# Banded attention and a cosine-gated MLP on one core: value differences in the first two blocks, paired bursts, later weight sums

## The chip, the core and the metric

The program runs on one core of one Trainium2 chip. The metric is the device time of one execution in microseconds; the kernel before takes 678.24 us (median of three runs, 677.9 to 679.14). The engines are named as the profile names them: PE multiplies matrices (PEld loads its weights), DVE, ACT and POOL work on vectors, SP issues the transfers.

## What is computed

Attention over a band of 96 keys and 8 global keys, for 4 batches of 8 heads, 768 positions and 64 columns, and then a two-layer network over all 3072 tokens of 512 columns with 2048 hidden ones:

```python
scores = scale * np.matmul(q, k.transpose(0, 1, 3, 2))
keep = is_global | is_local          # pos < 8, or 0 <= rel < 96
scores = np.where(keep, scores + bias, -1e9)
a = np.exp(scores - np.max(scores, axis=-1, keepdims=True))
x = np.matmul(a / (np.sum(a, axis=-1, keepdims=True) + 1e-09), v)
h = x @ w_in
out = (h * np.cos(h)) @ w_out
```

Inputs are float32; the kernel multiplies each matrix as a high and a low part, in three products.

## The kernel before

**Tiling.** The queries are cut into blocks of 96. A *part* is a run of blocks of one batch: batch 0 has parts 0 and 1 of four blocks each (`OPEN`), each later batch has parts of three, three and two blocks (`BLOCKS`), parts 2 to 10. A *unit* is one part and one pair of heads, so a part has four units. `plan_unit` makes the scores of a unit (lines 663 and 667), folds the two 96-key windows into one (line 685), takes row minima (694), the exponentials with their sums (ACT, 719), adds 1e-9 to the sums (DVE, 727), inverts them (730) and normalises by groups of two blocks (743 and 748, on POOL or DVE). `plan_values` transposes the probabilities on PE (847), copies them from PSUM into two halves of a `pv` tile, and multiplies them by V in a *burst* (`av`, line 890) that uses 64 columns of the array for each head.

**Two ways to split the probabilities.** After the fold one column holds a key of the block before or one of the own block, by the mask `own`. Without differences (parts 0 to 3) DVE makes two masked copies: `others` (line 858) and `own` (864). With differences (`DIFFER`, parts 4 to 10) the first half is a plain copy (`every`, line 855, ACT or DVE, shown as line 297 or 299), the second is `own`, and its products use V of the own block less V of the block before (`vd`, line 821, POOL or DVE). `vd` has one slot, `pv` has three.

**Bursts.** The parts of two blocks put two units into one burst (`both`, `off`), the others one. A burst's result goes to a PSUM bank `px`, from which `plan_x` makes the high part of x (ACT, 297) and the low one (DVE, 938). From part 4 on the attention has two banks ("att"); parts 1 to 3 have three ("wide").

**The network.** `plan_opening` and `plan_step` multiply x by `w_in` (line 973), make the cosine on ACT and DVE (991 to 1104) and multiply by `w_out` (986). From part 3 on, a tile of 256 tokens is multiplied in seven products instead of eight (`plan_fast`, line 1191), with sums of weights that `plan_combined` makes once (lines 496 to 522), stores in DRAM and reads back. `plan_weight` converts the weights from 64-bit words in six steps on ACT, DVE and POOL; line 456 (`wjoin`) puts the words together and 466 (`wrest`) is the last step. `plan_store` copies a finished tile of the plain steps to an `oo` tile and stores it; its slot is of class "wu" for part numbers under `FAST` = 3, else "oo". "wu" is two of the four slots "late", which the sums and the fast steps use as well; "oo" has two slots.

**Order.** All engines take their instructions in the order of a list that `Plan.run` writes: each operation has a cost for every engine that may do it, a due time, slots for its buffers, and a place on the engine that is free first. In the first 110 us (`HURRY`) ACT's costs count half and DVE's double. Where the plan finds a gap on PE in the first 45 us, it puts in products of zeros (line 1518). These stand in no data path.

Of the kernel before, what the change touches and what calls it, by code (L numbers as in the profile page):

```python
# [18 lines left out]
ALU = mybir.AluOpType  # L19
# [7 lines left out]
R = 96  # L27
# [9 lines left out]
UB = 1  # L37
# [11 lines left out]
PE, ACT, DVE, POOL, SP = "PE", "ACT", "DVE", "POOL", "SP"  # L49
# [14 lines left out]
FAST = 3  # L64
SUMS = -5

MERGE = tuple(range(11, 11))
DIFFER = tuple(range(4, 11))
# [3 lines left out]
TAIL = 0.8  # L72

# [32 lines left out]
class Plan:  # L106
# [12 lines left out]
    def __init__(self, places, free):  # L119
        self.ops = []  # L120
        self.places = {c: list(v) for c, v in places.items()}
        self.busy = {}
        self.free = dict(free)
        self.port = 0
        self.mode = None
        self.last = {}

# [5 lines left out]
    def op(self, engines, emit, after=(), uses=(), due=None, table=None, extra=0, port=False, mode=None):  # L133
        o = Op(engines, emit, after, list(uses), due, table, extra, port, mode)
        for a in o.after:
            a.then.append(o)
        for u in o.uses:
            u.users += 1
        self.ops.append(o)
        return o  # L140
# [13 lines left out]
    def run(self):  # L154

        self.dues()
        for i, o in enumerate(self.ops):
            o.key = (o.due - min(o.engines.values()), i)
# [114 lines left out]
class Net:  # L273
# [143 lines left out]
    def plan_weight(self, src, out, at, place, n, due):  # L417

        nc, p = self.nc, self.plan
        raw = Slot(f"w {place}", lambda i: self.const.tile([P, n, 2], U32, name="raw", tag=i))  # L420
# [53 lines left out]
        o = p.op({DVE: part(600)}, wjoin, [o], [raw, wu], port=True)  # L474
        o = p.op({ACT: part(525), DVE: part(335), POOL: part(595)}, whigh, [o], [raw, wu], port=True)
        return p.op({DVE: part(600), POOL: part(1260)}, wrest, [o], [raw, wu], due=due, port=True)

    def plan_combined(self, q):
# [11 lines left out]
        done = [[x] + self.prev.get("sums", []) for x in done]  # L490
# [99 lines left out]
    def plan_unit(self, L, pr):  # L590
# [134 lines left out]
        def add(e):  # L725
            x = st.tile[:, n2 : 2 * n2]
            nc.vector.tensor_scalar(x, x, 1e-9, None, op0=ALU.add)

        def rec(e):
            nc.vector.reciprocal(st.tile[:, 2 * n2 : 3 * n2], st.tile[:, n2 : 2 * n2])  # L730

        o = p.op({DVE: 85}, add, exps, [st], port=True)
        o = p.op({DVE: 120}, rec, [o], [st], port=True)
        u["norm"] = []
        for ts in groups:
            h, na = ts[0], 2 * len(ts)

            def norm(e, h=h, na=na):
                x = tt[h // 2].tile.rearrange("p t j w -> p (t j) w")[:, :na]
                r = st.tile[:, 2 * n2 + 2 * h : 2 * n2 + 2 * h + na].rearrange("p (c o) -> p c o", o=1)  # L740
                if lead(h):
                    for a, w in ((0, R), (2, SLOT)):
                        self.eng(e).tensor_tensor(
                            x[:, a : a + 2, :w], x[:, a : a + 2, :w],
                            r[:, a : a + 2].broadcast_to([R, 2, w]), op=ALU.mult,
                        )
                    return
                self.eng(e).tensor_tensor(x, x, r.broadcast_to([R, na, SLOT]), op=ALU.mult)  # L748
# [51 lines left out]
    def plan_values(self, u):  # L800
# [18 lines left out]
        def step(e):  # L819
            x = vs.tile[:R, :, hs]  # L820
            self.eng(e).tensor_tensor(
                vd.tile[:, pos + lead0 : pos + nb], x[:, lead0 + 1 : nb + 1], x[:, lead0:nb], op=ALU.subtract)
# [6 lines left out]
        for ts in u["groups"]:  # L829
# [37 lines left out]

            def whole(e, pt=pt, pv=pv):
                self.copy(e, pv.tile[:R, 1, : 2 * R], pt.tile[:R, : 2 * R])
# [7 lines left out]
            ready.append(p.op({DVE: 70 + w * 104 // 100}, own, [o], [pt, pv]))  # L877
# [28 lines left out]
        def burst(e):  # L906
# [4 lines left out]
            {PE: 160 * (2 * nb - u["first"]) * len(units)}, burst, [o for x in units for o in x[3]],  # L911
# [87 lines left out]
    def plan_step(self, s, m, q, a, b):  # L999
# [10 lines left out]
        for i in range(2):  # L1010
            f = 2 * q + i
            for kk in range(self.NK):

                def m1(e, kk=kk, f=f, i=i):
# [3 lines left out]
                    {PE: 348}, m1, self.xdone[m, kk] + [self.wdone[f][0]], [ph, *xs, self.weight["wi", f]],  # L1018
# [100 lines left out]
    def plan_fast(self, s, m, q, rr, gg, product, g, due):  # L1119
# [54 lines left out]
        for i, (bank, half, left, right, k) in enumerate(jobs):  # L1174
# [12 lines left out]
            def times(e, b=b, half=half, left=left, right=right, ends=half == 1 or bank == "D"):  # L1187
# [7 lines left out]
                {PE: 348}, times, after, uses + side, due=due + (i + 1) * 348,  # L1195
# [65 lines left out]
    def plan_store(self, m, t, po, o, keep, due):  # L1261
# [3 lines left out]
        if before is not None:  # L1265
            oo = before[0]
        else:
            cls = "part" if keep else "wu" if m < FAST else "oo"
            oo = Slot(cls, lambda i: self.work.tile([P, 512], F32, name="oo", tag=i))
# [175 lines left out]
    def windows(self):  # L1445
# [17 lines left out]
        self.weight, self.saved, self.stored = {}, {}, {}  # L1463
        p = self.plan
# [13 lines left out]
        for n in self.order:  # L1478
            for b2 in range(self.NP // UB):
                L = self.plan_loads(n, b2)  # L1480
                for i in range(UB):
                    self.plan_values(self.plan_unit(L, b2 * UB + i))
        for f in range(self.NF):
            self.wdone[f] = self.plan_weights(f)
        for q in range(NQ):
            self.plan_combined(q)
        for s, (n, i, a, b) in enumerate(self.seq):
            (self.plan_opening if n < len(OPEN) else self.plan_step)(s, n, i, a, b)
        flag = self.plan_flag()
# [105 lines left out]
```

## Time and profile before

| | before |
|---|---|
| median of three runs | 678.24 us |
| span of the profiled execution | 676.7 us |
| PE busy | 663.8 us (98%) |
| DVE busy | 554.6 us (82%) |
| ACT busy | 508.7 us (75%) |
| POOL busy | 391.0 us (58%) |

The span runs from the first to the last instruction; the run's time has 1.5 us around it. A matmul's record lasts longer than the step from its start to the next one's, since matmuls overlap: to see what PE spends on one, subtract starts. In a timeline a row is a run of equal instructions: start, time from the first start to the last end, and how many. The brackets give the idle time before it and what ended that.

### The profile page before, as it was taken

To read this page: it belongs to the slowest core of one execution; us is meant where nothing else is said; L and a number is where in the kernel's file an instruction comes from. 1 tells how busy PE (TensorE), PEld (TensorE's weight loads), DVE (VectorE), ACT (ScalarE), POOL (GpSimd) and SP (SyncE) were. 2 spreads that over 40 slices of the span, in tenths; PEclk is the share of its full clock that TensorE was granted. 3 is DMA by queue.
4 is the path that set the end of the run, shared out by engine and by line. 5 is a ranking of instruction groups with operands and counts; after the bars stand their busy time and mean duration, and the time that the engine had idled before them with its cause. 6 is when DMAs were issued, how large, how long until landed. Compare 5 with 4: busy or idle time off the path is not lost. (4 is left out here: it accounts for less than half of the span.)

```text
span 676.7 us, 17496 instructions
## 1 busy us (share of the span) xinstructions
PE 663.8 (98%) x5810; PEld 626.7 (93%) x5810; DVE 554.6 (82%) x1726; ACT 508.7 (75%) x1253; POOL 391.0 (58%) x576
## 2 busy tenths in 40 slices
PE   8999999999999999999999999999999999999995
PEld 4769999999999998999999999999999999999995
DVE  7999898978898897777778888797878898887664
ACT  7999997579776785866778878676787788684432
POOL 5896544437457553467866776736876768532201
PEclk9999999999999999999999999999999999999999
DMA  8999200044546665877887867787687777665664
GB/s 279 336 321 380 80 1 1 22 159 121 163 139 194 221 183 174 239 220 203 244 240 207 249 213 231 245 239 232 210 240 219 235 228 235 199 224 187 191 226 150
DMA packets 86291, 136.69 MB, mean 202 GB/s; under 512 B 9904, under 2 KB 33968, under 8 KB 86192
## 3 DMA queue, kind: packets, MB, share of 16 engines
q1 hardware_dynamic: 86048, 135.23, 64.7%
q8 instruction: 48, 0.79, 0.5%
q14 instruction: 51, 0.42, 0.2%
q10 hardware_dynamic: 144, 0.26, 0.1%
HBM read 118.67 MB, written 16.78 MB: 200 GB/s over the span
## 5 line engine op out<-in xcount | busy, mean ns | idle before, releaser
L973 PE MATMUL bank<-xmem,w 128*128 128x256 f32 (+1 forms) x2112 | 344.4, 295 | 0.1
L973 PEld LDWEIGHTS bank<-xmem,w 128*128 128x128 f32 x2112 | 294.1, 189 | 7.7 <-issue 0.9
L719 ACT ACTIVATE tt<-tt,st 96x104 f32<-96x104 f32 (+1 forms) x256 | 94.6, 371 | 7.2 <-DVE st L694 6.5
L997 ACT ACTIVATE rr<-rr,half_pi 128x512 f32<-128x512 f32 (+1 forms) x104 | 71.6, 691 | 23.3 <-DVE rr L994 22.1
L986 PE MATMUL bank<-w,gh 128*128 128x256 f32 (+1 forms) x384 | 88.3, 320 | 0.0
L991 ACT ACTIVATE rr<-bank 128x512 int32<-128x512 f32 (+1 forms) x104 | 57.9, 558 | 30.9 <-PE bank L973 29.1
L1191 PE MATMUL bank<-ws,sh 128*128 128x256 f32 x384 | 75.8, 284 | 1.3 <-DVE oo L299 1.3
L994 DVE SCALAR_TENSOR_TENSOR rr<-rr,bank 128x512 f32<-128x512 int32 (+1 forms) x104 | 66.5, 639 | 8.2 <-ACT rr L991 7.6
L784 POOL TENSOR_TENSOR qk<-raw,qk 64x304 fp32r<-64x304 f32 (+1 forms) x57 | 50.0, 880 | 28.4 <-ACT qk L297 6.9
L748 POOL TENSOR_TENSOR tt<-tt,st 96x416 f32<-96x416 f32 (+1 forms) x60 | 45.4, 764 | 35.3 <-DVE sf L1137 9.1
L986 PEld LDWEIGHTS bank<-w,gh 128*128 128x128 f32 x384 | 62.7, 188 | 1.1
L1030 DVE TENSOR_TENSOR rr<-bank,rr 128x512 f32<-128x512 f32 x72 | 49.3, 684 | 16.6 <-ACT rr L997 16.4
L986 PE MATMUL bank<-w,gl 128*128 128x256 f32 (+1 forms) x192 | 61.1, 318 | 0.0
L1191 PEld LDWEIGHTS bank<-ws,sh 128*128 128x128 f32 x384 | 58.6, 188 | 2.0 <-issue 1.4
L297 ACT CAST gh<-rr 128x384 fp32r<-128x384 f32 (+1 forms) x76 | 39.5, 520 | 25.8 <-DVE rr L1030 10.8
L694 DVE CUSTOM_DVE_ANT_0 tt<-bank,dd 96x104 f32<-96x104 f32 (+1 forms) x256 | 55.0, 256 | 2.2
L1191 PE MATMUL bank<-ws,sl 128*128 128x256 f32 x192 | 54.1, 282 | 0.1
L997 ACT ACT_TABLE_LOAD x40 | 51.3, 1283 | 0.7
L719 ACT ACT_TABLE_LOAD x39 | 50.0, 1283 | 0.7
L445 POOL TENSOR_SCALAR raw<-raw 128x512 bf16<-128x512 bf16 (+1 forms) x32 | 36.6, 1167 | 23.6 <-DVE w L466 13.2
L667 PE MATMUL bank<-qk 128*96 128x200 f32 (+1 forms) x384 | 49.1, 257 | 0.0
L1191 PE MATMUL bank<-w,gh 128*128 128x256 f32 x256 | 48.7, 282 | 0.0
(137 smaller groups left out, 1532.4 us busy)
## 6 DMA issues: line engine op xcount, KB each, us to landing
ws<-sum SPq DMA_DIRECT2D x256, 256.0 KB
raw<-in_qk_dram SPq DMA_DIRECT2D x48, 174.0 KB
raw<-in_w_in_dram SPq DMA_DIRECT2D x16, 512.0 KB
sum<-sw SPq DMA_DIRECT2D x64, 128.0 KB
raw<-in_qk_dram SPq DMA_DIRECT2D x48, 150.0 KB
raw<-in_qk_dram SPq DMA_DIRECT2D x48, 148.0 KB
out_dram<-oo SPq DMA_DIRECT2D x23, 256.0 KB
raw<-in_w_out_dram SPq DMA_DIRECT2D x16, 256.0 KB
```

The lines of the kernel that those rows point to most:

```text
L667: nc.tensor.matmul(out, qs[:, m, q0], ks[:, k : k + w], start=m == 0, stop=m == 1)
L694: nc.vector.tensor_tensor_reduce(tt[t // 2].tile[:, t % 2, j, :w], ps.tile[:R, i * WIN : i * WIN + w], self.dd[:, v, :w], op0=ALU.add, op1 ...
L719: nc.scalar.activation(x, x, AF.Exp, bias=st.tile[:, c : c + 1], scale=-1.0, accum_out=st.tile[:, n2 + c : n2 + c + 1])
L748: self.eng(e).tensor_tensor(x, x, r.broadcast_to([R, na, SLOT]), op=ALU.mult)
L784: self.eng(e).tensor_tensor(ks[D:, k0:k1], raw.tile[D:, k0:k1], ks.bitcast(F32)[D:, k0:k1], op=ALU.subtract)
L973: self.nc.tensor.matmul(ph, self.wi[f][:, w, kk * P : (kk + 1) * P], xx[:, kk, :], start=kk == 0 and m == 0, stop=kk == self.NK - 1 and m ...
L986: self.nc.tensor.matmul(out, gg, w[:, i, :], start=start and m == 0 and h == 0, stop=stop and m == 2)
L991: self.nc.scalar.activation(r.bitcast(I32), ph, AF.Copy, scale=1.0 / TWO_PI, bias=0.25)
L994: self.nc.vector.scalar_tensor_tensor(r, r.bitcast(I32), -TWO_PI, ph, op0=ALU.mult, op1=ALU.add)
L997: self.nc.scalar.activation(r, r, AF.Sin, bias=self.half_pi)
L1030: {DVE: dve(512)}, lambda e: nc.vector.tensor_tensor(r(), h(), r(), op=ALU.mult), [o], [ph, rr],
L1191: nc.tensor.matmul(out, x, y, start=q == 0 and j == 0 and half == 0, stop=q == self.NF // 2 - 1 and j == 2 and ends)
```

## The change

- `DIFFER` takes in parts 0 and 1, so that their probabilities are split with value differences. `step` counts V's blocks from the first that is loaded.
- `APART`: in parts 0 and 1 the sums and reciprocals are made for each group of two blocks, each after its own four exponentials, and not once for the unit's eight.
- `MERGE`: parts 2 to 10 pair two units in a burst. In the parts of three blocks the second unit has a bank of its own; the odd blocks of both share a `pv` tile.
- `BEHIND`: in the plan the first weight sum waits for the last 24 joins.
- Part 2 stores from slots of class "oo".
- The planner counts 354 ns for a group of three products instead of 348, and 168 instead of 160 for a pair of products with V.
- Names of operations, `ORDER` and `COPIED` are added; they are empty.

```diff
-MERGE = tuple(range(11, 11))
-DIFFER = tuple(range(4, 11))
+BEHIND = -24
+MERGE = tuple(range(2, 11))
+DIFFER = (0, 1) + tuple(range(4, 11))
+COPIED = ()
+APART = (0, 1)
...
+ORDER = {}
...
-            o.key = (o.due - min(o.engines.values()), i)
+            o.key = (o.due - min(o.engines.values()) + ORDER.get(o.name, 0), i)
...
         o = p.op({DVE: part(600)}, wjoin, [o], [raw, wu], port=True)
+        self.joined.append(o)
...
-        done = [[x] + self.prev.get("sums", []) for x in done]
+        done = [[x] + self.prev.get("sums", self.joined[BEHIND:]) for x in done]
...
-        def add(e):
-            x = st.tile[:, n2 : 2 * n2]
+        def add(e, a, b):
+            x = st.tile[:, n2 + a : n2 + b]
             nc.vector.tensor_scalar(x, x, 1e-9, None, op0=ALU.add)
 
-        def rec(e):
-            nc.vector.reciprocal(st.tile[:, 2 * n2 : 3 * n2], st.tile[:, n2 : 2 * n2])
-
-        o = p.op({DVE: 85}, add, exps, [st], port=True)
-        o = p.op({DVE: 120}, rec, [o], [st], port=True)
+        def rec(e, a, b):
+            nc.vector.reciprocal(st.tile[:, 2 * n2 + a : 2 * n2 + b], st.tile[:, n2 + a : n2 + b])
+
+        ends = None
         u["norm"] = []
         for ts in groups:
             h, na = ts[0], 2 * len(ts)
+            if n in APART or ends is None:
+                cs = (2 * h, 2 * h + na) if n in APART else (0, n2)
+                ends = [x for ((t, _), _), x in zip(ttr, exps) if t in ts or n not in APART]
+                o = p.op({DVE: 85}, lambda e, cs=cs: add(e, *cs), ends, [st], port=True)
+                o = p.op({DVE: 120}, lambda e, cs=cs: rec(e, *cs), [o], [st], port=True)
...
-                vd.tile[:, pos + lead0 : pos + nb], x[:, lead0 + 1 : nb + 1], x[:, lead0:nb], op=ALU.subtract)
+                vd.tile[:, pos + lead0 : pos + nb], x[:, lead0 + 1 - low : nb + 1 - low], x[:, lead0 - low : nb - low], op=ALU.subtract)
...
-            {PE: 160 * (2 * nb - u["first"]) * len(units)}, burst, [o for x in units for o in x[3]],
+            {PE: 168 * (2 * nb - u["first"]) * len(units)}, burst, [o for x in units for o in x[3]],
...
-                    {PE: 348}, m1, self.xdone[m, kk] + [self.wdone[f][0]], [ph, *xs, self.weight["wi", f]],
+                    {PE: 354}, m1, self.xdone[m, kk] + [self.wdone[f][0]], [ph, *xs, self.weight["wi", f]],
...
-                {PE: 348}, times, after, uses + side, due=due + (i + 1) * 348,
+                {PE: 354}, times, after, uses + side, due=due + (i + 1) * 348,
...
-            cls = "part" if keep else "wu" if m < FAST else "oo"
+            cls = "part" if keep else "wu" if m < FAST - 1 else "oo"
```

## Rows read from the trace of the kernel before

**Rows 1.** page section 1: busy us (share of the span) xinstructions.

```profile
PE 663.8 (98%) x5810; PEld 626.7 (93%) x5810; DVE 554.6 (82%) x1726; ACT 508.7 (75%) x1253; POOL 391.0 (58%) x576
```

**Rows 2.** busy time by stretch: us, busy us (x instructions) of each engine.

```profile
0.00:62.00 62.00, 58.34 (x556) 41.30 (x557) 54.65 (x258) 57.20 (x191) 47.01 (x82) 1.00 0.96 324
60.00:80.00 20.00, 20.00 (x143) 18.69 (x143) 17.47 (x31) 20.00 (x43) 10.06 (x11) 1.00 0.64 215
```

**Rows 3.** the same for line 1518 alone, 5.75 to 62 us.

```profile
5.75:62.00 56.25, 9.74 (x38) 3.35 (x38) 1.00 1.00 342
```

**Rows 4.** timeline of PE, opening: start us, us, engine line, operation [idle before].

```profile
8.49 3.41 PE L1518 MATMUL idle<-zeros 128*128 128x512 bf16 x15
12.05 0.51 PE L847 MATMUL bank<-ident,tt 96*96 96x96 f32 x4
29.93 1.83 PE L973 MATMUL bank<-xmem,w 128*128 128x384 f32 x9
```

**Rows 5.** timeline of PE round one burst, 468.9 to 470.9 us.

```profile
468.99 0.28 PE L1191 MATMUL bank<-ws,sl 128*128 128x256 f32 x1
469.10 0.51 PE L973 MATMUL bank<-xmem,w 128*128 128x256 f32 x3
469.54 0.56 PE L890 MATMUL bank<-pv,v 96*64 96x96 f32 x8
470.09 0.34 PE L890 MATMUL bank<-pv,v 104*64 104x96 f32 x4
470.26 0.34 PE L890 MATMUL bank<-pv,vd 96*64 96x96 f32 x4
470.52 0.50 PE L1191 MATMUL bank<-w,sh 128*128 128x256 f32 x2
```

**Rows 6.** timeline of PE, two waits of transposes.

```profile
285.93 0.54 PE L847 MATMUL bank<-ident,tt 96*104 96x96 f32 x4 [0.23 <-POOL tt L748]
...
321.72 0.35 PE L847 MATMUL bank<-ident,tt 96*104 96x96 f32 x2 [0.71 <-DVE pv L299]
```

**Rows 7.** timelines of ACT, SP's queue, DVE and PE, 263 to 271 us.

```profile
263.57 0.59 ACT L297 COPY oo<-bank 128x512 f32<-128x512 f32 x1
264.66 5.69 SPq L1283 DMA_DIRECT2D out_dram<-oo  x2
269.27 0.69 DVE L299 COPY oo<-bank 128x512 f32<-128x512 f32 x1 [1.92 <-DMA out_dram<-oo]
270.11 0.48 PE L1191 MATMUL bank<-ws,sh 128*128 128x256 f32 x2 [1.27 <-DVE oo L299]
```

**Rows 8.** timelines of DVE and POOL, last join and first weight sum.

```profile
129.91 0.42 DVE L456 SCALAR_TENSOR_TENSOR wu<-raw 128x256 uint32<-128x256 uint32 x1
132.51 0.75 POOL L496 TENSOR_TENSOR sw<-w 128x256 f32<-128x256 f32 x1 [0.80 <-DVE qk L774]
```

**Rows 9.** instructions by line, DVE, 0 to 62 us: busy us, mean ns | idle before.

```profile
L858 DVE SCALAR_TENSOR_TENSOR pv<-own,bank 104x384 f32<-104x384 f32 (+1 forms) x16 | 7.9, 496 | 1.4 <-PE bank L847 0.8 <-ACT pv L297 0.4
L730 DVE RECIPROCAL st<-st 96x8 f32<-96x8 f32 x8 | 1.6, 195 | 0.1
L727 DVE TENSOR_SCALAR st<-st 96x8 f32<-96x8 f32 x8 | 1.4, 174 | 0.3 <-ACT tt L719 0.3
```

**Rows 10.** instructions by line and shape, ACT and POOL, whole span.

```profile
L297 ACT COPY pv<-bank 104x384 f32<-104x384 f32 x15 | 7.1, 476 | 3.7 <-DVE pv L864 3.6
L297 ACT COPY pv<-bank 104x192 f32<-104x192 f32 x18 | 5.4, 318 | 4.7 <-PE bank L847 2.5 <-DVE pv L864 2.0
L821 POOL TENSOR_TENSOR vd<-v 96x384 f32<-96x384 f32 x7 | 7.1, 1011 | 4.3 <-PE bank L667 2.9 <-PE bank L973 1.3
```

**Rows 11.** timelines of ACT and POOL, first unit.

```profile
8.70 0.18 ACT L719 ACTIVATION_READ_ACCUMULATOR tt<-tt,st 96x1 f32 x1
10.15 0.19 ACT L719 ACTIVATION_READ_ACCUMULATOR tt<-tt,st 96x1 f32 x1
11.05 0.99 POOL L743 TENSOR_TENSOR tt<-tt,st 96x192 f32<-96x192 f32 x2 [2.20 <-ACT tt L719]
```

More of the change, by code (lines that the diff above doesn't have):

```diff
@@ L126, in __init__ @@
         self.last = {}
+        self.part, self.count = "", {}
     def drained(self, o, e):
@@ L134, in op @@
         o = Op(engines, emit, after, list(uses), due, table, extra, port, mode)
+        name = emit.__name__
+        if name == "<lambda>":
+            self.count[self.part] = self.count.get(self.part, 0) + 1
+            name = f"op{self.count[self.part]}"
+        o.name = f"{self.part} {name}"
         for a in o.after:
@@ L419, in plan_weight @@
         nc, p = self.nc, self.plan
+        p.part = place
         raw = Slot(f"w {place}", lambda i: self.const.tile([P, n, 2], U32, name="raw", tag=i))
@@ L866, in own, with mine @@
                 )
+            def mine(e, pv=pv, a=a, na=na, z0=z0):
+                self.eng(e).tensor_tensor(
+                    wide(pv.tile[:R, 1, z0:], a, na), wide(pv.tile[:R, 0, z0:], a, na), mask(self.own[:R], a, na), op=ALU.mult
+                )
             def whole(e, pt=pt, pv=pv):
@@ L876, in plan_values @@
                 ready.append(p.op({DVE: 70 + w * 104 // 100}, others, [o], [pt, pv]))
-            ready.append(p.op({DVE: 70 + w * 104 // 100}, own, [o], [pt, pv]))
+            if n in COPIED:
+                ready.append(p.op({DVE: 70 + w * 104 // 100, POOL: 100 + w * 1125 // 512}, mine, ready[-1:], [pv], port=True))
+            else:
+                ready.append(p.op({DVE: 70 + w * 104 // 100}, own, [o], [pt, pv]))
             if lead:
@@ L1463, in windows @@
         self.weight, self.saved, self.stored = {}, {}, {}
+        self.joined = []
         p = self.plan
@@ L1479, in windows @@
             for b2 in range(self.NP // UB):
+                p.part = f"v{n}.{b2}"
                 L = self.plan_loads(n, b2)
                 for i in range(UB):
+                    p.part = f"u{n}.{b2 * UB + i}"
                     self.plan_values(self.plan_unit(L, b2 * UB + i))
         for f in range(self.NF):
+            p.part = f"w{f}"
             self.wdone[f] = self.plan_weights(f)
         for q in range(NQ):
+            p.part = f"c{q}"
             self.plan_combined(q)
         for s, (n, i, a, b) in enumerate(self.seq):
+            p.part = f"s{s}"
             (self.plan_opening if n < len(OPEN) else self.plan_step)(s, n, i, a, b)
+        p.part = "flag"
         flag = self.plan_flag()
```

## The prediction

> **What bounds the kernel now.** I read the page's busy shares first, then the busy time by stretch, then the timeline of PE. The reader is to see that PE is busy 98% of the span [rows 1]: nearly every microsecond that another engine saves is worth nothing unless PE gets its work sooner or has less of it. The profiled execution spans 676.7 us, and the median of the runs is 678.24 us, so some 1.5 us lie outside the span; I make the sum on the span's rows and subtract it from the median.
>
> The stretches say where PE's time is not useful work. From 60 us on PE is full (20.00 of 20 us to 80 us) [rows 2], and by the page's 98% nearly so to the end: what is saved there has to be PE's own time, or one of a few waits. In the first 62 us PE is busy 58.34 us [rows 2], but 13.65 us of these cannot be useful: the matmuls of line 1518 multiply zeros to keep PE running where the plan sees a gap. After the first score matmul (5.75 us) they hold 9.74 us [rows 3]. With the truly idle time, 62 - 58.34 = 3.66 us, that is 13.4 us of the opening that more speed elsewhere could win at the very most. In the same stretch ACT is busy 57.20 and DVE 54.65 of 62 us, POOL 47.01 [rows 2]: ACT is the fullest of the three, POOL has room.
>
> **The bursts: twelve fewer changes of PE's array shape.** A burst (line 890) uses 64 columns of the array for each head, the work around it all 128. The timeline shows both edges. Before: one 128-column matmul advances PE by 0.11 us (468.99 to 469.10), the next three take from 469.10 to 469.54 = 0.44 us instead of 3 x 0.117 = 0.35: 0.09 us for going in. After: four matmuls take 0.17 us inside the burst (470.09 to 470.26), the last four take 0.26 (470.26 to 470.52): 0.09 us for going out [rows 5]. So a burst costs 0.18 us besides its products. By the code the parts of three blocks (2, 3, 5, 6, 8, 9) have 6 x 4 = 24 bursts now and 12 after; the parts of two blocks are paired already. The gain is 12 x 0.18 = 2.2 us, all of it PE's own time and so of the span. No products are added or dropped. Bounds: no less than nothing from this alone, 2.2 at most.
>
> What pairing adds: the even unit's PV tiles, its V tile and the difference tile wait for the odd one, three `pv` slots are all held until the burst, and the burst needs both banks of "att" at once, since a pair of three-block units does not fit one. Queued behind it on PE in the plan are the next unit's scores and transposes, which need these banks; they come free when ACT and DVE have copied x out. MoE matmuls stand between, so I cost the hold at nothing where the plan has such work, and at one wait of PE where it has not. Nearest rows: the transposes ahead of one of the six bursts that are paired already waited 0.23 us, and the longest wait of PE for a copy to `pv` in the fast parts was 0.71 us [rows 6]. For 18 bursts that is between 0 and 18 x 0.71 = 12.8 us; by the six paired ones 18 x 0.23 / 6 = 0.7 us. I take 0.7, since they are the same mechanism with the same slots, and keep the other end for a rival. A replanned order can also lose a wait that it has now, so this cost could lie some tenths below nothing.
>
> The Trainium skill's page "TensorEngine Tiling (Array Packing)", section Performance Considerations, holds that tiling speeds up the array but not the emptying of PSUM, so that the copies may become the bottleneck. That speaks against bigger bursts: with the rule deciding, a pair's wait would be the 0.71 us of the row and not the tenth of a microsecond that I take, and the sum would lose its gain. The paired bursts in this trace do not show it; no run yet shows it for pairs that fill both banks.
>
> **The store tiles of part 2: one wait goes.** `plan_store` now takes "oo" instead of "wu" from part 2 on. The wait is in the timeline: ACT copies the first half out (263.57), SP stores it (264.66), and DVE's copy of the second half at 269.27 waited for that store to land, 1.92 us, because both halves got one and the same slot; the matmuls of line 1191 queued on PE behind the bank stood idle 1.27 us [rows 7]. Class "oo" has two slots, and by the code no other user between the last stores of parts 0 and 1 and the first outputs of part 3, so the second copy needs no store. Gain 1.3 us; bounds 0 (the copy itself comes late) and 1.3. What is late next there is DVE's angle step, with a copy of 0.69 us before it.
>
> **The weight sums.** They now wait, in the plan, for the last 24 joins. In the trace before, the first sum starts at 132.51 us and the last join at 129.91 [rows 8]: the order is already so, and nothing changes. Cost 0. If the joins came later, sums would too; they feed the fast parts, which begin by 270 us [rows 7], and over 130 us of cover lie between.
>
> **The first two blocks.** Value differences remove line 858 on DVE: 16 instructions of mean 496 ns, 7.9 us. In their place come 16 plain copies, on ACT by the plan's weights in this stretch: 4 units of (0.318 + 0.476) and 8 copies of 0.476 = 3.2 + 3.8 = 7.0 us [rows 9, 10]. New are 8 differences: 384 elements took POOL 1.01 us [rows 10], so 512 some 1.35; 4 x 1.01 + 4 x 1.35 = 9.4 us, if POOL does them, out of its 15 idle. They need only V and the one `vd` slot, which the burst before frees; the next unit's burst must then come at least 1.01 or 1.35 us later, and its own products, transposes and scores lie between. New are also 8 more pairs of sum and reciprocal, 8 x (0.174 + 0.195) = 3.0 us on DVE [rows 9]. Balance over 62 us: DVE -7.9 + 3.0 = -4.9, ACT +7.0, POOL +9.4. ACT has 62 - 57.20 = 4.8 us idle: at least 2.2 us of its weight conversion must go to DVE, which has the room, or past 62 us.
>
> What the halves buy: in the first unit the fourth exponential's sum ends at 8.88 us and the eighth's at 10.34; normalising on POOL starts at 11.05 only after the eighth, and PE's zeros fill 8.49 to 12.05 [rows 4, 11]. With its own sum and reciprocal the first half can start 10.34 - 8.88 = 1.46 us sooner. In later units the normalisation, not the exponential, decides, and a lighter DVE lets the first weights be joined sooner: the first MoE matmul starts at 29.93 [rows 4], right after the first weight's last step. I take 2.0 us for the whole opening: 1.5 for the first unit, and 0.5 of the later gaps. Its bounds are far apart: 13.4 us won at the top, and at the bottom 7.0 - 4.8 = 2.2 us lost if ACT's surplus passes on to PE in full.
>
> The planner's costs (354 for 348, 168 for 160) remove no instruction; they shift the order by under 2%, counted with the 0.7 above.
>
> **Sum.** 2.2 + 1.3 + 2.0 - 0.7 = 4.8 us. 678.24 - 4.8 = 673.4 us.
>
> **The rivals.**
> Opening wins nothing: ACT's added copies eat what the halves give. 678.24 - 2.2 - 1.3 + 0.7 = 675.4. For it: ACT's 57.20 of 62; against it: weights may go to DVE, and PE has zeros to drop.
> Opening wins more: the earlier weights fill half of the 9.74 us of zeros, 4.9 + 1.5 instead of 2.0: 669.0. For it: DVE is the engine with the longest queue ahead of the joins; against it: ACT is not relieved at all.
> New waits eat the gain: a replanned order leaves two or three more waits of 0.7 to 1.3 us on PE, as it has now at 270 and 321 us [rows 6, 7]: near 677.3, within the bound of no change. This is also how it looks if pairing does not do what it says, because the freed 0.18 us come back as a wait ahead of each burst.
> Slower by ACT's backlog: all 7.0 us of copies stay on ACT, which is full up to 80 us besides (20.00 of 20) [rows 2], the weights come that much later, and PE, which takes them in order, stands for it: 678.24 - 3.5 + 0.7 + 7.0 - 1.5 = 680.9. It decides from the point where weights arrive later than PE asks for them; PE is full from 60 to 80 us in the trace, so some lead is there.
> Slower by banks: each of the 12 new pairs waits 0.71 us: 673.4 + 8.5 = 681.9. It decides from 0.4 us a pair (4.8 / 12). Against it: the MoE matmuls between.
>
> **How the numbers follow.** Forecast 673.4 with 0.45; opening wins more 0.15; opening wins nothing 0.17; new waits 0.11; ACT's backlog 0.08; banks 0.04. About 0.2% is what a measurement of this kernel can tell from no change, 1.4 us. The first three cases are faster: 0.77; new waits, no change: 0.11; the last two, slower: 0.12. The range leaves out the backlog and the banks and the far end of the opening's gain: 668.8 to 678.6.
>
> **What would show it.** Line 890 in 26 groups instead of 38, and 0.18 us less for each. No wait of line 1191 for a copy to `oo` near 265 us. Line 858 with 16 instructions instead of 32, and `vd` written before 62 us. Fewer or shorter zeros after 5.75 us: the 9.74 us should come down by about 2; if they stay, the opening's term is wrong, and if ACT is full while PE waits for weights between 62 and 140 us, the backlog decides. Waits of transposes or scores for `pv` and banks past 150 us above 0.7 us in sum would make the pairing's price wrong.

## The result, and the profile after

| | before | after |
|---|---|---|
| time, median (lowest to highest) | 678.31 us (677.9 to 679.14) | 682.86 us (682.26 to 683.4) |
| ratio, 95% interval | 1 | 1.0064 (1.005 to 1.0078) |
| profiled execution: its time, its span | 679.14, 676.7 us | 682.26, 679.8 us |

The changed kernel is slower by 0.64%; forecast were 4.8 us won, measured are 4.55 us lost. (The 678.24 us of the prediction is the median of three of these four runs of before.) The two profiled executions happen to be the slowest of before and the fastest of after, so the traces have only 3.1 of these 4.55 us to explain. Around each of the two spans lie 2.4 us; the 1.5 us named ahead compared the median with the span of the slowest run.

First the page's busy shares of after and its busy time by stretch (columns as in [rows 1] and [rows 2]):

```profile
PE 662.9 (98%) x5805; PEld 626.1 (92%) x5805; DVE 567.7 (84%) x1782; ACT 503.4 (74%) x1265; POOL 372.5 (55%) x526
...
0.00:62.00 62.00, 56.15 (x533) 38.88 (x535) 53.49 (x260) 56.42 (x193) 41.77 (x79) 1.00 0.95 321
60.00:80.00 20.00, 19.73 (x141) 18.16 (x141) 19.58 (x34) 19.40 (x42) 9.85 (x9) 1.00 0.69 227
```

PE is 98% busy as before [rows 1], with less in it, and the span is longer. In the first 62 us PE is busy 56.15 us instead of 58.34 [rows 2]; POOL has lost 5.2 us of work there, while DVE over the span has gained 13.1 us (554.6 to 567.7).

Where the time went I count on PE's timeline: for each matmul the time to the start of the next one, less what its shape takes where nothing waits (0.175 us for 128x384, 0.117 for 128x256). The start of the 241st 128x384 matmul of the first MoE layer (20 steps of 12) is the mark for the opening: 126.1 us before, 129.8 after.

| | before | after | difference |
|---|---|---|---|
| opening, to the mark | 126.1 | 129.8 | +3.7 |
| changes of the array's shape, all bursts | 8.0 | 5.7 | -2.3 |
| the wait for the store at 269 us, on PE | 1.4 | 0 | -1.4 |
| other waits and rest (what remains to 3.1) | | | +3.1 |

Both gains that I had worked out from rows are there; the opening lost where I had put a gain, and what remains, waits for the most part, is four times the 0.7 us that I had allowed for new waits. Up to the mark both kernels run the same matmuls, zeros aside: PE's idle time there rose from 3.7 to 6.5 us, the zeros fell from 13.7 to 12.7, and the same matmuls took 1.8 us longer in sum.

The timeline of PE in the opening, first two rows of before, then after (columns as in [rows 4]):

```profile
55.64 0.50 PE L986 MATMUL bank<-w,gh 128*128 128x256 f32 x2
...
61.74 0.73 PE L986 MATMUL bank<-w,gh 128*128 128x512 f32 x2
```

```profile
8.51 2.33 PE L1550 MATMUL idle<-zeros 128*128 128x512 bf16 x10
10.99 0.51 PE L864 MATMUL bank<-ident,tt 96*96 96x96 f32 x4
...
28.47 1.32 PE L998 MATMUL bank<-xmem,w 128*128 128x384 f32 x6
...
54.41 2.36 PE L998 MATMUL bank<-xmem,w 128*128 128x384 f32 x12
58.37 0.54 PE L864 MATMUL bank<-ident,tt 96*104 96x96 f32 x4 [1.61 <-POOL tt L765]
...
62.80 1.84 PE L998 MATMUL bank<-xmem,w 128*128 128x384 f32 x9 [0.27 <-DVE rr L1121]
64.48 0.63 PE L1011 MATMUL bank<-w,gh 128*128 128x512 f32 x2
```

It begins as forecast: the first transposes start at 10.99 instead of 12.05, the first MoE matmul at 28.47 instead of 29.93 [rows 4]. Then the lead is given back. Compare equal work: burst 7 and the 12 products next to it are done at 55.64 us before (start of line 986 after them) and at 56.60 after (the last product starts at 56.42 and takes 0.175); burst 8 and its 9 products at 61.74 before and at 64.48 after. Of these 2.7 us, 1.61 are one wait of the transposes for a normalisation. The other engines round it (timeline, after):

```profile
55.84 0.69 DVE L838 TENSOR_TENSOR vd<-v 96x512 f32<-96x512 f32 x1
56.30 0.40 ACT L308 CAST w<-wu 128x256 fp32r<-128x256 f32 x1
56.45 0.17 DVE L743 RECIPROCAL st<-st 96x4 f32<-96x4 f32 x1
56.60 0.46 ACT L308 COPY pv<-bank 104x384 f32<-104x384 f32 x1
56.76 0.72 POOL L478 TENSOR_TENSOR w<-wu,w 128x256 fp32r<-128x256 f32 x1 [2.85 <-ACT w L308]
57.45 0.87 POOL L765 TENSOR_TENSOR tt<-tt,st 96x416 f32<-96x416 f32 x1
```

POOL stood idle for 2.85 us with the normalisation (line 765) behind a weight step (line 478) that waited for a cast on ACT; the reciprocal that line 765 needs came late as well, behind a value difference on DVE. All three engines are in this wait.

The groups of DVE, 5.75 to 62 us, after (columns as in [rows 9]):

```profile
L881 DVE TENSOR_TENSOR pv<-bank,own 96x384 f32<-96x384 f32 (+1 forms) x16 | 8.0, 501 | 1.5 <-ACT pv L308 1.1 <-PE bank L864 0.3
...
L838 DVE TENSOR_TENSOR vd<-v 96x384 f32<-96x384 f32 (+1 forms) x6 | 3.7, 613 | 0.0
L740 DVE TENSOR_SCALAR st<-st 96x4 f32<-96x4 f32 x16 | 3.6, 223 | 0.8 <-ACT tt L732 0.8
...
L743 DVE RECIPROCAL st<-st 96x4 f32<-96x4 f32 x16 | 2.7, 169 | 0.1
...
L310 DVE COPY pv<-bank 104x384 f32<-104x384 f32 x3 | 1.6, 543 | 0.0
```

Six of the eight differences are on DVE, two on POOL (1.00 and 1.28 us); of the 16 copies 13 are on ACT and 3 on DVE. DVE's balance here is -7.9 (line 858 [rows 9]) + 3.7 + 1.6 + (3.6 + 2.7 - 3.0) = +0.7 us, where I had reckoned -4.9. And line 881 now waits for ACT's copy of the same bank, 1.1 us: before, both readers of a transposed bank were DVE's, the first block's aside.

ACT is no fuller than before, although it has 5.4 us of the new copies: 56.42 of the first 62 us, and from 20 to 60 us 38.98 of 40 (before 39.71, shown below):

```profile
20.00:60.00 40.00, 36.62 (x355) 26.78 (x352) 36.16 (x156) 38.98 (x122) 26.74 (x34) 1.00 0.98 334
```

What gave way is the conversion of the weights. Its first step on ACT (line 435, now 447) ran 16 times in the first 62 us before and 7 times after; its last step (line 466, now 478) ran 9 times before, 6 times after. No wait of PE up to 150 us is put down to a weight, so what this delay costs is not shown.

### The profile page after: what moved, and what is told of

It is laid out like the page before. It is cut to its first block, busy times and chain, and to the rows that moved or that the text cites. A ratio compares the mean times of both kernels' runs of the same rounds, so it can differ in the third digit from the quotient of the medians.

```text
span 679.8 us, 17477 instructions
## 1 busy us (share of the span) xinstructions
PE 662.9 (98%) x5805; PEld 626.1 (92%) x5805; DVE 567.7 (84%) x1782; ACT 503.4 (74%) x1265; POOL 372.5 (55%) x526
## 4 chain that ended last, share of the span: by engine, by line
PE 69%; ACT 12%; DVE 9%; DMA 5%; POOL 2%; issue 2%; SPq 0%; POOLq 0%; DVEq 0%; ACTq 0%
PE bank L998 30%; PE bank L1216 19%; PE bank L1011 8%; PE bank L680 5%; PE bank L915 5%; DMA raw<-in_qk_dram 2%; PE bank L864 2%; ACT raw L447 2%; ACT rr L1022 2%; ACT raw L463 1%; ACT w L308 1%; ACT tt L732 1%; DMA raw<-in_w_out_dram 1%; DVE rr L1055 1%; DMA raw<-in_w_in_dram 1%
## 5 line engine op out<-in xcount | busy, mean ns | idle before, releaser
L732 ACT ACTIVATE tt<-tt,st 96x104 f32<-96x104 f32 (+1 forms) x256 | 94.7, 371 | 13.1 <-DVE st L707 12.6
L1011 PEld LDWEIGHTS bank<-w,gh 128*128 128x128 f32 x384 | 62.5, 188 | 1.0
L1216 PEld LDWEIGHTS bank<-ws,sh 128*128 128x128 f32 x384 | 58.5, 188 | 1.2 <-DVE oo L1235 0.6
L801 POOL TENSOR_TENSOR qk<-raw,qk 64x304 fp32r<-64x304 f32 (+1 forms) x53 | 46.6, 886 | 21.9 <-DVE qk L791 9.5
L308 ACT CAST sh<-sf 128x512 fp32r<-128x512 f32 x40 | 24.8, 619 | 37.1 <-DVE sf L1162 28.7
L680 PE MATMUL bank<-qk 128*96 128x200 f32 (+1 forms) x384 | 50.5, 257 | 1.0 <-POOL qk L801 0.7
L312 POOL TENSOR_SCALAR gh<-rr 128x384 fp32r<-128x384 f32 (+1 forms) x40 | 22.1, 552 | 52.3 <-DVE sf L1162 36.9
L457 POOL TENSOR_SCALAR raw<-raw 128x256 bf16<-128x256 bf16 (+1 forms) x31 | 32.5, 1065 | 32.7 <-DVE gl L1129 9.5
L698 DVE COPY_PREDICATED bank<-mine,bank 96x192 f32<-96x192 uint32 (+1 forms) x128 | 40.4, 328 | 9.6 <-PE bank L680 8.0
```

What stands on the lines that cost most here:

```text
L680: nc.tensor.matmul(out, qs[:, m, q0], ks[:, k : k + w], start=m == 0, stop=m == 1)
L732: nc.scalar.activation(x, x, AF.Exp, bias=st.tile[:, c : c + 1], scale=-1.0, accum_out=st.tile[:, n2 + c : n2 + c + 1])
L801: self.eng(e).tensor_tensor(ks[D:, k0:k1], raw.tile[D:, k0:k1], ks.bitcast(F32)[D:, k0:k1], op=ALU.subtract)
L1011: self.nc.tensor.matmul(out, gg, w[:, i, :], start=start and m == 0 and h == 0, stop=stop and m == 2)
L1216: nc.tensor.matmul(out, x, y, start=q == 0 and j == 0 and half == 0, stop=q == self.NF // 2 - 1 and j == 2 and ends)
```

## The experiments

The theories: A, the copies added on ACT delay the opening; B, pairs wait for banks and copies; C, any edit makes the planner draw the whole order anew, and the waits that the new order happens to have decide; D, order is of no account. Later two finer ones for the opening: E, the difference step on DVE lies in the chain; F, handing a transposed bank from ACT to DVE costs. "Opening" below is the mark at the 20th step.

**One edit of the change undone, planned anew.**

```diff
undo_differ   DIFFER = tuple(range(4, 11))
undo_apart    APART = ()
undo_merge    MERGE = tuple(range(11, 11))
undo_costs    {PE: 354} -> {PE: 348} (twice), {PE: 168 * ...} -> {PE: 160 * ...}
```

> The changed kernel with the value differences of the first two blocks undone, all else kept. Its measured time is 682.86 us, and the trace puts 3.7 us of the 4.5 us of loss ahead of the first network step that follows the opening's 16 steps on part 1 (126.1 us before, 129.8 after). Theory A, added copies on ACT delay the opening: 679 us, with that step back near 126. Theory B, the pairing and its waits cost it: 682 to 683. Theory C, the time follows no single edit because every edit rewrites the whole order: anywhere from 677 to 684, with waits at other places than in the changed kernel.

> The changed kernel with one sum and one reciprocal for each unit again in the first two blocks, all else kept. Theory A (ACT's added copies): 683 to 685, since the halves only help. If the 16 small DVE instructions more (3.0 us) are what delays the opening: 680. Theory B (pairing): 682 to 683. Theory C (any edit rewrites the order): 677 to 684.

> The changed kernel with single bursts in the parts of three blocks again, all else kept. If the pairing is worth its 12 x 0.18 us and no more: 685. Theory B, its waits cost more than that: 680 to 682, with the waits of PE past 300 us gone. Theory A: 684 to 685. Theory C: 679 to 686.

> The changed kernel with the planner's old costs (348 and 160) again, all else kept; no instruction is added or removed by it but zeros of the opening. My prediction put this edit at nothing: 682 to 684. Theory C (any edit rewrites the order): 677 to 686, as far off as an undone edit that removes work.

| | time | ratio (95%) | opening | array changes |
|---|---|---|---|---|
| undo_differ | 682.63 | 1.0062 (1.0045 to 1.0078) | 128.3 | 5.3 |
| undo_apart | 687.82 | 1.0148 (1.0131 to 1.0166) | 135.8 | 5.3 |
| undo_merge | 683.83 | 1.0084 (1.0068 to 1.0101) | 129.6 | 8.4 |
| undo_costs | 684.27 | 1.0091 (1.0074 to 1.0108) | 130.8 | 5.2 |

No edit, taken out, wins the loss back: without the differences the time is the same, without any one of the other three the time is longer still. Only the array changes do what the edit says: some 3 us more without pairing. Even the costs, which touch no instruction, shift the time by 1.4 us. The openings spread over 7.5 us. That speaks for C and against A and B alone, though undo_apart lies above all its ranges, C's 677 to 684 too. In two of the traces PE's clock has a part in it: after stretches in which PE was busy 1.67 and 2.34 of 4 us, the granted clock was 0.51 from 53 to 56.5 us (undo_apart) and 0.57 from 58.5 to 62.5 us (undo_costs) of the 2.4 GHz level, so at 1.2 GHz for most of these stretches. In before and after it is 1.00 until the last 4 us.

**One planner price moved by one nanosecond, no instruction changed.**

```diff
before_exp366, after_exp366   exps.append(p.op({ACT: 365}, ...  ->  {ACT: 366}
before_av161                  {PE: 160 * (2 * nb - ...          ->  {PE: 161 * (2 * nb - ...
after_av169                   {PE: 168 * (2 * nb - ...          ->  {PE: 169 * (2 * nb - ...
```

> The kernel before, in which the planner counts 366 ns for an exponential instead of 365. No instruction is added, removed or changed but for zeros of the opening and the engine that a movable step runs on; only the order is written anew. Theory C (the kernel before has a lucky order, and any new order costs some us): 680 to 685. Theory D (the order is of no account, and the change itself costs 4.5 us): 677.5 to 679.

> The kernel before, in which the planner counts 161 ns instead of 160 for a pair of products with V. Theory C: 680 to 685, and not the same waits of PE as with the exponential's nanosecond. Theory D: 677.5 to 679.

> The changed kernel with 366 ns for an exponential instead of 365. Theory C: anywhere from 677 to 687; if the edits are worth what my sum says besides the order (2.2 us of array changes, 1.3 of the store tiles), then by that less than the kernel before with the same nanosecond. Theory D: 682 to 684.

> The changed kernel with 169 ns instead of 168 for a pair of products with V. Theory C: anywhere from 677 to 687, not the same waits as with the exponential's nanosecond. Theory D: 682 to 684.

Measured: before_exp366 703.83 (1.0386, 1.0368 to 1.0403), before_av161 678.72 (1.0013, 1.0004 to 1.0023), after_exp366 692.74 (1.0221, 1.0194 to 1.0247), after_av169 687.89 (1.0151, 1.0133 to 1.0168). One nanosecond in a price is worth 0.7 to 25.8 us (before_av161 and before_exp366 against the 678.01 us of before beside them; after_av169 and after_exp366 are 5.0 and 9.9 us above after). So D, that the order is of no account, falls, and C holds in kind. But none of the four times lies in the range that I had given to C: three lie above it, and before_av161 lies in D's. Timelines of PE and POOL in before_exp366, and its busy time by stretch:

```profile
78.97 0.88 PE L847 MATMUL bank<-ident,tt 96*104 96x96 f32 x4 [11.52 <-POOL tt L748]
...
56.37 1.39 POOL L445 TENSOR_SCALAR raw<-raw 128x512 bf16<-128x512 bf16 x1
78.04 0.88 POOL L748 TENSOR_TENSOR tt<-tt,st 96x416 f32<-96x416 f32 x1 [20.28 <-DVE wu L456]
...
40.00:60.00 20.00, 19.14 (x177) 15.12 (x174) 18.35 (x71) 19.78 (x54) 15.52 (x21) 1.00 0.95 332
60.00:80.00 20.00, 8.33 (x48) 6.96 (x46) 19.20 (x34) 20.00 (x40) 0.88 (x1) 0.75 0.65 207
80.00:100.00 20.00, 15.71 (x94) 14.36 (x95) 16.15 (x35) 19.27 (x47) 10.15 (x12) 0.66 0.03 9
```

POOL did nothing for 20.28 us: in this order its normalisation stands behind a run of weight joins on DVE (the plan orders such a POOL step behind a DVE step that uses the shared port), and PE waited 11.52 us for it. Neither of the two neighbours of before is faster than it, and one is far slower. An edit that is planned anew is compared with this one draw, not with an average order; two neighbours are too few to say how good a draw it is. To price the edits I kept the old order in the next runs and put the edit in behind the planner.

**The old order kept: the store tile.** After the plan, the second stores' slots of part 2 are renamed to class "oo"; nothing else moves.

```diff
+            if m == 2: self.moved.append((oo, f"oo{t}"))
+        ops = p.run()
+        for slot, at in self.moved: slot.at = at
```

> The kernel before, its order kept to the letter: only the two store tiles of part 2 are moved to the two slots oo0 and oo1 after the order is written. My sum put this at 1.3 us, the wait at 270 us. If that term was right and only the new order spoilt it: 676.7 (0.998). If another wait takes its place (DVE's angle step behind the copy): 677.5 to 678.

676.89 us (0.9982, 0.9973 to 0.9991): 1.3 us won, as worked out from [rows 7]. In its trace the second copy starts without a wait:

```profile
266.95 0.68 DVE L299 COPY oo<-bank 128x512 f32<-128x512 f32 x1
```
This run beats both kernels, and the edit is the one part of the change that is worth keeping as it stands.

**The old order kept: the first two blocks.** The joins become plain copies on ACT, or on DVE; the eight differences stand on DVE ahead of each unit's first copy.

```diff
+        for o, every, step in self.grafts:
+            o.emit, o.engine = every, ACT        # old_order_dve_copies: DVE
+            if step is not None:                 # ahead of o, engine DVE
+                ops.insert(ops.index(o), step_op)
```

> The kernel before, its order kept, with the value differences of the first two blocks put in by hand: each masked copy of line 858 becomes a plain copy on ACT at the same place in the order, and each unit's difference is made on DVE just ahead of its first copy. Nothing else is written anew. Theory A (ACT's added 7 us delay the opening): 681 to 685, with the first step after part 1's sixteen at 129 to 133 us instead of 126.1, and ACT without gaps ahead of it. Theory C (the edit is harmless, its new order costs): 677.5 to 679.5.

> As the run with the copies on ACT, but with the plain copies on DVE, where the masked ones were: ACT has as much to do as before, DVE 8 x 0.5 = 4 us more for the differences. Theory A: 678 to 680, since ACT is relieved against the other run; if DVE is what binds the opening: 681 to 682. Theory C: 677.5 to 679.5.

683.18 (1.0074, 1.0061 to 1.0087) and 684.09 us (1.008, 1.0067 to 1.0093). The order is the old one, so C alone does not explain the opening: the edit itself, put in at these places, costs some 5 us. But A alone does not either, since the copies on DVE are no better; their 684.09 us lie above every range that I had set. The two ingredients one by one:

```diff
old_order_copies_no_step   copies on ACT, no differences (the products take the own block's v)
old_order_step_alone       joins as before, eight differences on DVE that nobody reads
old_order_step_pool        copies on ACT, the differences on POOL at the same place
old_order_halves           for ts in groups: add, reciprocal of that half only, at the old place
```

> The kernel before in its old order, with plain copies on ACT in place of the 16 joins of the first two blocks (as in the run with the old order and copies on ACT), but without the eight value differences; the products take the own block's v where the difference would stand, so the values of the first blocks are not those of the reference. Theory E (the difference step lies on DVE's queue ahead of the reciprocals and copies, and DVE is in the chain of the opening): with the step gone DVE has 7.9 us less work than before, and the time is 676 to 679. Theory F (handing the transposed bank from ACT to DVE costs: DVE's own copy waits for ACT's, 5.7 us in ten waits): 681 to 683, as with the differences. Both in half: 680.

> The kernel before in its old order with its joins on DVE as they are, and eight value differences added on DVE ahead of the first join of each unit of the first two blocks; nothing reads them. Theory E: eight times 0.56 to 0.86 us on the opening's chain, 682 to 684.5. Theory F: the handing over is absent, so DVE's slack takes the steps: 678 to 679.5.

> The kernel before in its old order, copies on ACT, and the eight value differences on POOL instead of DVE at the same place in the order; the computation is the reference's. Theory E: DVE is relieved of 7.9 us and POOL takes 8 x 1.0 to 1.3 us; POOL normalises for the same chain, so part of it is paid: 677 to 681. Theory F: 681 to 683.5. My price in the prediction, which put the differences on POOL at nothing, would give 678 or less.

> The kernel before in its old order, sums and reciprocals of the first two blocks cut in halves at the place where they stand, so that eight more pairs of short instructions run on DVE and nothing starts sooner. The added pairs are 8 x (0.22 + 0.17) = 3.1 us of DVE. Theory E: most of it is paid, 680 to 681.5. Theory F or an opening set by the order alone: 678 to 679.

| | time | ratio (95%) | opening |
|---|---|---|---|
| old_order_copies_no_step | 682.62 | 1.0068 (1.0051 to 1.0084) | 130.9 |
| old_order_step_alone | 682.28 | 1.0058 (1.0041 to 1.0075) | 131.4 |
| old_order_step_pool | 685.42 | 1.0104 (1.0087 to 1.0121) | 133.1 |
| old_order_halves | 678.59 | 1.0003 (0.9994 to 1.0013) | 126.4 |

Each ingredient costs some 4 us by itself (4.3 and 4.0; both together 4.9, so the delays do not add), and the halves cost nothing: they add 1.1 us of DVE's time up to 66 us, not the 3.1 that I had reckoned, and the 680 to 681.5 us of E for them failed. The busy time from 20 to 60 us, first of before, then of copies_no_step, with the longest wait of DVE in the latter (0 to 66 us):

```profile
20.00:60.00 40.00, 38.52 (x385) 29.77 (x385) 37.45 (x158) 39.71 (x121) 34.95 (x40) 1.00 0.99 337
```

```profile
20.00:60.00 40.00, 36.73 (x357) 26.62 (x356) 29.80 (x140) 39.83 (x127) 30.70 (x36) 1.00 0.91 303
...
DVE pv L867 <- ACT pv L297: 11.8, 15, 1.5
```

ACT was full before (39.71 of 40) and is full now, DVE has 7.65 us less to do, and nobody gains: DVE stands 11.8 us behind ACT's copies: its read of a transposed bank waits for ACT's, and ACT's copy sits in its queue, mostly right behind an exponential. That is A and F in one: the bank is handed over by the fullest engine. (The Trainium skill, "Advanced Engine Details and Errata", section Bank Collisions, says that the engines cannot access the same PSUM bank within one partition on the same cycle. The trace does not test that: in the 15 waits DVE's reader starts only on a semaphore that follows ACT's copy, and no run here shows what an overlap would do.)

For the step alone, the fifth burst of before, then timelines of DVE, POOL and PE in old_order_step_alone:

```profile
39.03 1.55 PE L890 MATMUL bank<-pv,v 104*64 104x96 f32 x32
```

```profile
36.04 1.72 POOL L748 TENSOR_TENSOR tt<-tt,st 96x416 f32<-96x416 f32 x2
37.45 2.10 DVE L824 TENSOR_TENSOR vd<-v 96x512 f32<-96x512 f32 x1
37.72 1.28 POOL L466 TENSOR_TENSOR w<-wu,w 128x512 fp32r<-128x512 f32 x1
...
40.63 0.88 PE L663 MATMUL bank<-raw 64*96 64x200 f32 x6 [1.17 <-DVE pv L867]
41.51 2.53 PE L895 MATMUL bank<-pv,v 104*64 104x96 f32 x32
...
47.58 0.68 DVE L824 TENSOR_TENSOR vd<-v 96x512 f32<-96x512 f32 x1
```

A difference takes 0.68 us alone. This one took 2.10: it began while POOL was still normalising (line 748), and ended 0.55 us after POOL's next step of 1.28. It is one of eight; the others took 0.54 to 0.96 us. The joins queue behind it, PE waits 1.17 us for them, and the fifth burst starts at 41.5 instead of 39.0. E holds for the differences. (The Trainium skill, "SBUF — State Buffer", section SBUF: two separate sides, has it that GpSimd and a VectorE instruction with two inputs in SBUF share a port pair, which one of them holds for a whole instruction while the other is blocked. This row agrees, in that DVE ended only after both of POOL's steps.) This execution is the slowest of its four and overstates the loss: after a stretch in which PE was busy 3.33 of 4.5 us, the granted clock was 0.57 of the 2.4 GHz level from 41.5 to 45.5 us, and the burst took 2.53 us instead of 1.55. On POOL the step is dearer still, 685.42, above the ranges of both theories: there it delays the normalisations, and PE waits 3.8 us for them up to 70 us (1.1 before, up to 66).

**Pairing.**

```diff
only_pairing    all as before, MERGE = tuple(range(2, 11))
pairing_av161   the same with {PE: 161 * (2 * nb - ...
undo_opening    after, with DIFFER = tuple(range(4, 11)) and APART = ()
```

> The kernel before with the pairing alone (parts 2 to 10), all other settings old; the order is written anew, the opening's attention is that of before. Its own worth by the sum is 2.2 us of array changes less 0.7 of waits: 676.5. Theory B (pairs that fill both banks wait): 679 to 685 with waits of scores or transposes for banks past 150 us. Theory C: anywhere from 676 to 690, with 12 bursts less all the same, and the loss at places that have nothing to do with bursts.

> Pairing alone (parts 2 to 10, all else as before), with the planner's price for one product of a burst at 161 instead of 160 ns; the same step moved the kernel before by 0.4 us. If pairing itself costs (theory B: pairs wait for copies and banks), the time is again 680.5 to 681.5, some 2.8 over before. If the 2.8 us are waits that this one order happens to have (theory C), the time differs from 681.0 by more than 1 us in either direction, and could lie at 676 to 679, where the 2.3 us of array changes would show.

> The changed kernel with both edits of the first two blocks undone (no value differences and no half sums there); pairing, store tiles, costs and the wait of the sums stay. If the opening's loss comes from these edits, the twentieth step of the first weights comes back from 129.8 to about 126.5 us and the span loses 3.3 us: 679 to 680. By the sum of my prediction without the opening's term: 675.4. Theory C (any new order may lose): anything from 676 to 684, with the opening at 126 to 131 us whatever was undone.

681.02 (1.0044, 1.0028 to 1.006), 682.1 (1.0058, 1.0038 to 1.0077) and 690.77 us (1.0186, 1.0167 to 1.0204). In both runs of pairing alone the opening is the old one (126.1 and 126.3), the array changes fall to 5.4 us, and the time is 2.8 and 3.6 us longer than that of before beside them. That fits B, but the neighbour does not decide between B and C as I had meant it to: 682.1 lies above the 680.5 to 681.5 that I had given to B, and 1.1 us from 681.0, which I had counted for C; and the intervals of the two ratios overlap. The busy time from 300 to 660 us of before, after and only_pairing, in this order:

```profile
300.00:660.00 360.00, 359.10 (x3355) 352.65 (x3355) 288.14 (x892) 259.40 (x622) 219.68 (x333) 1.00 0.74 223
```

```profile
300.00:660.00 360.00, 357.35 (x3350) 351.52 (x3349) 295.80 (x934) 253.78 (x625) 195.36 (x281) 1.00 0.75 223
```

```profile
300.00:660.00 360.00, 355.66 (x3326) 348.80 (x3326) 292.73 (x918) 243.50 (x600) 201.31 (x294) 1.00 0.73 222
```

PE stands idle 0.90, 2.65 and 4.34 us. In all nine runs with pairing it is 2.5 to 5.0 us there; in the three that were planned anew without it, 0.8 (before_av161), 1.7 (before_exp366) and 2.8 (undo_merge). The eight bursts fewer in this stretch save 8 x 0.18 = 1.4 us; the idle time added is 1.75 and 3.44. DVE has 7.7 and 4.6 us more to do than before, POOL 24 and 18 less. One such wait in after, on the timelines of ACT, DVE and PE, and the sum of its kind in only_pairing from 300 us on:

```profile
476.13 0.32 ACT L308 COPY pv<-bank 104x192 f32<-104x192 f32 x1
476.48 0.35 DVE L310 COPY pv<-bank 96x192 f32<-96x192 f32 x1 [0.38 <-ACT pv L308]
476.75 0.68 DVE L1055 TENSOR_TENSOR rr<-bank,rr 128x512 f32<-128x512 f32 x1
477.58 0.94 PE L998 MATMUL bank<-xmem,w 128*128 128x256 f32 x6 [0.64 <-DVE rr L1055]
...
PE bank L998 <- DVE rr L1055: 2.3, 4, 0.6
```

DVE's copy for a pair waits for ACT's copy of the same bank; DVE's angle step (line 1055) is queued behind it, and MoE matmuls wait for that step to free their bank. In only_pairing each of the four stands behind DVE's copies to `pv`, and waits of scores make up another 2.1 us past 150 us. So the waits are mostly not where I had priced them, at the transposes, but at the MoE matmuls and the scores behind other work on DVE. undo_merge, with no pairs, has PE idle 2.8 us too, so a part is any new order's; how much is pairing's own stays open. The rule of the Trainium skill that the prediction weighed ("TensorEngine Tiling (Array Packing)", section Performance Considerations: emptying PSUM may become the bottleneck) comes nearer than I had let it: the 0.38 and 0.64 us here are waits behind copies out of PSUM, in the order of the queue.

undo_opening settles the opening the other way: with the first blocks' code as before but the rest of the change in place, the mark is at 135.7. PE's fourth burst before, then PE's timeline in undo_opening:

```profile
31.69 1.39 PE L890 MATMUL bank<-pv,v 96*64 96x96 f32 x28
```

```profile
23.78 1.39 PE L915 MATMUL bank<-pv,v 96*64 96x96 f32 x28
...
26.37 4.27 PE L1550 MATMUL idle<-zeros 128*128 128x512 bf16 x19
...
41.41 1.39 PE L915 MATMUL bank<-pv,v 96*64 96x96 f32 x28
```

The fourth burst comes at 41.4 instead of 31.7 (before) or 29.7 (after). My expectation of 126.5 failed, and so did 679 to 680 and C's 676 to 684. A part of the loss is the clock's: after PE had been busy 2.33 of 4 us, the granted clock was 0.51 from 51 to 58 us. The same code in the opening has now given marks of 125.8 to 126.5 (five runs), 135.7 and 147.4 (before_exp366), by the order and the clock that came with it.

## Why the prediction was wrong, step by step

**Array changes, 2.2 us: right.** 26 bursts instead of 38, 2.3 us less.

**Store tile, 1.3 us: right,** alone (old_order_oo, 1.3) and in the change (the wait of 1.27 us [rows 7] is gone).

**Weight sums, 0:** not tried by itself. In the trace of after the first sum starts at 136.05 us and the last join at 131.60, so the order of [rows 8] has stayed.

**The opening, 2.0 us won: wrong,** by 5.7 us; this is the step that failed. The first half unit did start 1.0 us sooner and the zeros after 5.75 us fell from 9.74 to 8.31 us, as I had said; but fewer zeros were not more work: PE's idle time up to the mark rose by 2.8 us. I had named the row that warns of it: ACT 57.20 of 62 us [rows 2]. From 20 to 60 us it was 39.71 of 40, and a stretch that long hides that 4.5 of its 4.8 idle us lay in the first 20. The copies, which I put at 7.0 us, went onto an engine with no room, in the chain: 5.4 us of them in the change, where the weights' conversion gave way, and all of them with the old order held, where they alone cost 4.3 us. I let the differences be free on POOL; six of eight went to DVE, at 0.54 to 0.69 us each in front of copies or reciprocals. In the old order they cost 4.0 us on DVE by themselves, and on POOL, beside the copies, 2.8 us more than the copies without them (685.42 against 682.62). And the balance counted busy time, as if DVE's 4.9 us saved could pay for ACT's 7.0: the chain runs through both in turn. My lower bound of 2.2 us lost came from the same balance; measured are 3.7 in the change and 4.9 with the order held.

**New waits, 0.7 us: wrong in size.** They are about 3 us, by what remains in the sum; PE's idle time from 300 to 660 us alone rose by 1.75. I took the waits of six paired bursts at the transposes; what comes late is DVE's work queued behind copies, the MoE step above all, and the waits that any new order has. The sentence that a replanned order could also lose a wait gave this term a symmetric error of some tenths; the runs give several microseconds, and no run that was planned anew is faster than before. Why all lie on that side is not shown.

**The planner's costs, nothing: wrong in kind.** They remove no instruction, but undone they move the time by 1.4 us, and one nanosecond moves it by up to 25.8.

**The rivals.** ACT's backlog, priced at 680.9, was the nearest in mechanism: copies_no_step shows what copies on a full ACT cost. But it is not the same: the loss there lies ahead of 62 us, in DVE's waits behind ACT, and the sign that I had named, PE waiting for weights between 62 and 140 us while ACT is full, is missing in after (PE busy 77.37 and ACT 69.72 of 78 us). The banks (681.9) came nearest by number, and only partly by mechanism, so that is in part luck. At 0.08 and 0.04 both were too small. The replanned order stood in a rival too, but with two or three waits of 0.7 to 1.3 us, and with the opening's gain left in; the runs show the plan redrawn everywhere.

So the 4.55 us: the edit of the first blocks is not cheap in any order tried (4.9 us in the old one; in the new one it is better than undoing it, 682.86 against 690.77), and the rest of the span loses in waits what the bursts and the store win. How the opening's 3.7 us split between edit and order cannot be told, since the two do not add: the cause of the edit's loss is shown in the old order, and for the change itself it is argued from the same waits in its trace.

## What to carry to other kernels

Where a planner writes the order, price an edit with the old order held and the edit put in behind the plan: only then is it the edit that is measured, at the place where it was put, and a one-nanosecond change of a price tells how far the order alone can move the time. Read the fullest engine's room in the stretch where the chain runs through it, not over the whole stage: work moved onto an engine at 39.7 of 40 us was paid here, although it took 7.65 us off another. For a step on DVE in a stretch where POOL is busy, look at its longest row too, and at what waits behind it: one difference of eight took 2.10 us.

## What the runs showed of the hardware that I had not expected

After PE had stood still for 11.52 us in before_exp366, its granted clock was 0.75 (60 to 80 us) and 0.66 (80 to 100 us) of the 2.4 GHz level as the mean of the stretch, so part of it at 1.2 GHz, and four transposes took 0.88 us instead of 0.54; from 100 us on it is 1.00 again. A long wait in the opening thus costs more than its length. Up to the mark PE's idle time is 19.4 us instead of 3.7 (the wait of 11.52 and others after it), the same matmuls took 5.2 us longer, and the kernel 25.8. A burst took 2.83 us instead of 1.55 at the lower clock (81.95 us). A difference of 512 elements took 2.10 us beside POOL's steps, three times its 0.68.
